# Two heads per value product, part of an output product in split precision, and two copies moved from ScalarE to VectorE

## The chip, the cores and the metric

The kernel runs on one core of a Trainium2 chip. The metric is the device time of one execution in microseconds; the time before is 1042.04 us, the median of three runs (1040.24 to 1042.3).

## The reference

Three stages follow one another. Attention: 4 batches, 8 heads, 576 positions, head dimension 64, with a mask by blocks of 64 (a query sees its own block and those before it).

```python
scores = scale * q @ k.T                      # masked where block_i < block_j
attn = softmax(scores)
x = (attn @ v) -> (2304 tokens, 512)
h = x @ w_in                                  # 512 -> 2048
x2 = (h - tanh(h)) @ w_out                    # 2048 -> 512
xn = x2 / rms(x2) * rms_g
out = (silu(xn @ w_gate) * (xn @ w_val)) @ w_out2     # 512 -> 1536 -> 512
```

## The kernel before, in words

The 2304 tokens are six groups of 384. Most products are made in *split parts*: each operand is the sum of a high and a low part of type fp32r, and three products (high by high, high by low, low by high) take the place of one product of float32 operands (`gemm_out`, L704 to L707). The weights arrive as 64-bit numbers and are turned into float32 words on ScalarE and VectorE (`convert`, L129 to L151): for split parts it also makes the high part (ScalarE, `rnd`, L102) and the low part (VectorE, `lo`, L107).

Attention comes in units: one batch and its first six or last three query blocks, times four pairs of heads. The units of groups 0 and 1 are *light*: they use plain float32 operands. A pair of heads passes through score steps ("s", `scores`: product L481, maximum L494 on VectorE, exponential L496 on ScalarE), transposes of the probabilities ("t", `transp`: L525 on TensorE, then a copy into `pp`, which is on VectorE for every third tile of unit 0 and on ScalarE for the others), and value products ("a", `av_light`, L570 to L584): for each head three products of 64 columns of weights with 384, 256 and 128 columns of probabilities (L578). Head 0 writes partitions 0 to 63 of a bank `t`, head 1 partitions 64 to 127. After the second head ScalarE copies the bank to `xh` and VectorE makes `xl`. A float32 product shows as two records in the trace.

Unit 0, the first batch, runs alone in the first 50 us, since the first hidden product needs its result; a few conversions of weights (EARLY, L650 on) are mixed in. From then on the steps of the next unit are put between the matrix products of the current group (`aslot`, L908 on, by a table of costs in `plan`, L366 to L391), so that unit 1 runs beside group 0, unit 2 and others beside group 1.

Each group walks 16 chunks of 128 hidden columns: hidden product L929 to L931 (12 products), tanh on ScalarE (L937), `gh`, and the output product `out1` (L710 to L724) into three accumulators one chunk later in group 0 and LAG = 2 chunks later in the other groups. Group 0's output product uses float32 operands (L715), one product per tile of 128 tokens instead of three. Its output weights are converted to float32, two chunks in one ring tile, and stored (w1f, L648); group 1 loads them again, splits them (`w1get`, L664 to L674, ScalarE `w<-st` and VectorE) and stores the split parts (w1d), which groups 2 to 5 load. TensorE's order is that of the code; on the other engines a scheduler orders the instructions.

## Time and profile before

| | before |
|---|---|
| median of three runs | 1042.04 us |
| the profiled execution's own time | 1042.98 us |
| its span, first to last instruction | 1041.1 us |
| mean granted TensorE clock | 0.996 |
| TensorE busy | 98% |
| VectorE, ScalarE, GpSimd busy | 71%, 64%, 33% |

Busy times of matmuls are sums of intervals whose ends are modelled and overlap; the distance between two starts tells how long TensorE was held. Idle time of an engine costs something only where another engine waits for it.

### The profile page before, as it was taken

Reading aid. Unit: us, or ns where it says so; the run is one execution under the profiler, and the core shown is the slowest. Engines: PE = TensorE matmul, PEld = TensorE weight load, DVE = VectorE, ACT = ScalarE, POOL = GpSimd, SP = SyncE. Lnnn points to the kernel's source line nnn. Section 1 sums busy time; section 2 is a strip of 40 time slices with the busy share of each in tenths; the row PEclk is TensorE's granted clock in tenths of the full one; section 3 lists DMA queues with packets and bytes.
Section 4 is the critical chain, followed back from the end, with each engine's and each line's share of the span. In section 5 each row is a group of like instructions: output and inputs, shape, how many; then the busy total and the mean of one; then the engine's idle time right before and its main releaser. Section 6 shows DMA issues by size and latency. Waiting matters only on the chain.

```text
span 1041.1 us, 17914 instructions
## 1 busy us (share of the span) xinstructions
PE 1023.0 (98%) x6014; PEld 934.2 (90%) x6014; DVE 736.3 (71%) x1489; ACT 666.3 (64%) x1533; POOL 342.9 (33%) x467
## 2 busy tenths in 40 slices
PE   8899999999999999999999999999999999999998
PEld 5676668999899989999999989999999999999998
DVE  5776558676777786668666988837866678666775
ACT  6877768787898887788868776624732247412253
POOL 5522111122343233324332624645211370111710
PEclk9999999999999999999999999999999999999999
DMA  9998799979787699857859989986697667876664
GB/s 224 269 340 267 252 280 274 287 219 265 222 234 199 152 267 292 229 188 256 294 161 365 383 321 355 347 324 248 225 331 295 247 217 260 287 297 236 250 231 134
DMA packets 190957, 274.03 MB, mean 263 GB/s; under 512 B 109456, under 2 KB 151184, under 8 KB 184464
## 3 DMA queue, kind: packets, MB, share of 16 engines
q1 hardware_dynamic: 190864, 272.87, 80.1%
q8 instruction: 48, 0.79, 0.3%
q14 instruction: 45, 0.37, 0.1%
HBM read 209.39 MB, written 63.44 MB: 262 GB/s over the span
## 4 chain that ended last, share of the span: by engine, by line
PE 86%; DVE 5%; ACT 4%; DMA 2%; issue 1%; POOL 1%; SPq 1%; DVEq 0%; ACTq 0%; POOLq 0%
PE t L929 6%; PE t L931 6%; PE t L930 5%; PE t L481 5%; PE gv L1026 5%; PE gv L1027 5%; PE gv L1025 5%; PE acc L705 4%; PE acc L707 4%; PE acc L706 4%; PE acc L715 4%; PE t L525 4%; PE ga L1025 3%; PE ga L1027 3%; PE ga L1026 3%; PE ga L707 2%
## 5 line engine op out<-in xcount | busy, mean ns | idle before, releaser
L929 PE MATMUL t<-xh,w 128*128 128x384 f32 x384 | 137.1, 357 | 0.1
L931 PE MATMUL t<-xh,w 128*128 128x384 f32 x384 | 129.6, 338 | 0.0
L930 PE MATMUL t<-xl,w 128*128 128x384 f32 x384 | 129.3, 337 | 0.0
L1027 PE MATMUL gv<-xh,ws 128*128 128x384 f32 x308 | 103.4, 336 | 0.0
L1026 PE MATMUL gv<-xl,ws 128*128 128x384 f32 x308 | 103.4, 336 | 0.0
L1025 PE MATMUL gv<-xh,ws 128*128 128x384 f32 x308 | 103.3, 336 | 0.0
L705 PE MATMUL acc<-w,gh 128*128 128x512 f32 x240 | 98.5, 410 | 0.4 <-DVE x2s L723 0.2
L496 ACT ACTIVATE pt<-pt,stat 128x64 f32<-128x64 f32 (+2 forms) x144 | 80.5, 560 | 26.8 <-DVE pt L494 26.3
L707 PE MATMUL acc<-w,gl 128*128 128x512 f32 x240 | 94.8, 395 | 0.3 <-DVE gl L107 0.3
L706 PE MATMUL acc<-w,gh 128*128 128x512 f32 x240 | 94.4, 393 | 0.0
L1079 ACT ACTIVATE gt<-c 128x384 f32<-128x384 f32 x29 | 15.3, 527 | 119.6 <-DVE c L1078 119.6
L494 DVE TENSOR_SCALAR_CACHE_REDUCE pt<-t 128x64 f32<-128x64 f32 (+2 forms) x144 | 64.2, 451 | 28.2 <-PE t L481 26.8
L1082 POOL TENSOR_TENSOR g<-va,vb 128x384 f32<-128x384 f32 x29 | 31.1, 1073 | 154.3 <-ACT va L1081 137.7
L929 PEld LDWEIGHTS t<-xh,w 128*128 128x128 f32 x384 | 72.3, 188 | 4.1 <-issue 0.7
L930 PEld LDWEIGHTS t<-xl,w 128*128 128x128 f32 x384 | 72.4, 189 | 2.3
L931 PEld LDWEIGHTS t<-xh,w 128*128 128x128 f32 x384 | 72.0, 188 | 0.0
L102 ACT ACTIVATE pp<-t 128x512 fp32r<-128x512 f32 (+6 forms) x152 | 63.4, 436 | 11.5 <-PE t L525 10.8
L525 PE MATMUL t<-ident,pt 128*128 128x128 f32 x400 | 65.6, 273 | 1.8 <-DVE xl L107 1.3
L107 DVE TENSOR_TENSOR pp<-t,pp 128x512 fp32r<-128x512 f32 (+3 forms) x112 | 55.2, 509 | 16.3 <-ACT pp L102 15.7
L107 DVE TENSOR_TENSOR gl<-gt,gh 128x384 fp32r<-128x384 f32 x80 | 53.9, 673 | 18.0 <-ACT gh L102 17.7
L525 PEld LDWEIGHTS t<-ident,pt 128*128 128x128 f32 x400 | 50.5, 140 | 16.0 <-issue 5.2
L107 POOL TENSOR_TENSOR vp<-vr,vp 128x640 fp32r<-128x640 f32 (+1 forms) x24 | 33.2, 1383 | 86.0 <-ACT vp L102 86.0
(209 smaller groups left out, 3123.0 us busy)
## 6 DMA issues: line engine op xcount, KB each, us to landing
ws<-w2d SPq DMA_DIRECT2D x26, 1792.0 KB, 7.3
w<-w1d_i SPq DMA_DIRECT2D x68, 512.0 KB, 5.1
ws<-wod SPq DMA_DIRECT2D x21, 1536.0 KB, 6.0
w<-w1d_o SPq DMA_DIRECT2D x52, 512.0 KB, 5.3
st<-in_moe_w_out SPq DMA_DIRECT2D x28, 512.0 KB, 5.0
w2d<-wc SPq DMA_DIRECT2D x9, 1024.0 KB, 7.5
st<-in_moe_w_in SPq DMA_DIRECT2D x16, 512.0 KB, 5.3
w1d_i<-w SPq DMA_DIRECT2D x16, 512.0 KB, 4.3
```

The costliest lines, as they stand in the source:

```text
L107: eng.tensor_tensor(out=o, in0=full, in1=hi.bitcast(F32), op=ALU.subtract)
L496: ACT.activation(out=pt[:, 0:keys], in_=pt[:, 0:keys], func=AF.Exp, scale=-1.0, bias=least, accum_out=st[:, 8 + ti:9 + ti])
L525: PE.transpose(t[:, (j - a) * 128:(j - a + 1) * 128], pt[:, j * 128:(j + 1) * 128], ident)
L705: PE.matmul(acc, lhsT=gh[:, c], rhs=wh, start=first, stop=False, skip_group_check=more)
L706: PE.matmul(acc, lhsT=gh[:, c], rhs=wl, start=False, stop=False, skip_group_check=more)
L707: PE.matmul(acc, lhsT=gl[:, c], rhs=wh, start=False, stop=last, skip_group_check=more)
L929: PE.matmul(h, lhsT=wh[:, c], rhs=xh[:, kk], start=(kk == 0), stop=False)
L930: PE.matmul(h, lhsT=wh[:, c], rhs=xl[:, kk], start=False, stop=False)
L931: PE.matmul(h, lhsT=wl[:, c], rhs=xh[:, kk], start=False, stop=(kk == KD - 1))
L1025: PE.matmul(ps, lhsT=wh[:, c], rhs=xh[:, kk], start=(first and kk == 0), stop=False)
L1026: PE.matmul(ps, lhsT=wh[:, c], rhs=xl[:, kk], start=False, stop=False)
L1027: PE.matmul(ps, lhsT=wl[:, c], rhs=xh[:, kk], start=False, stop=(last and kk == nk - 1))
```

## The change

Three edits. (1) A light value step is one step for both heads: the products of the two heads alternate, head 0 and head 1 for each block of 128 keys, into one bank. (2) With SPLIT = 12, chunks 12 to 15 of group 0 use split parts in the output product: their output weights are converted with high and low part, one chunk per ring tile, and stored as split parts at once; the activation is split as well, and the lag is 2 chunks there. Group 1 loads these four chunks' weights instead of splitting them. (3) In unit 0 the copies of tiles 2 and 5 of each pair go from ScalarE to VectorE.

```diff
--- before.py
+++ after.py
@@ -51,6 +51,7 @@
 JH = J2 // 2
 MIXED = range(3, 10)
 LAG = 2
+SPLIT = 12
 AVLEAD = 3
 
 
@@ -377,7 +378,7 @@
                     period.setdefault(m, ([], [], []))[0].extend(("s", i, t) for t in half)
                     period.setdefault(m + 2, ([], [], []))[1].extend(("t", i, t) for t in half)
                     m += 1
-                period.setdefault(m + 2, ([], [], []))[2].extend(("a", i, hh) for hh in range(2))
+                period.setdefault(m + 2, ([], [], []))[2].extend(("a", i, hh) for hh in range(1 if u.light else 2))
             for n in sorted(period):
                 sc, tr, av = period[n]
                 self.seq += sc[0:2] + av + tr[0:1] + sc[2:3] + tr[1:]
@@ -386,7 +387,7 @@
                 u = self.pairs[n][0]
                 if kind == "a":
                     self.end[u.group] = m + 1
-                self.cost.append(self.cost[-1] + (u.tiles[t][0] + 150 if kind in "st" else 400))
+                self.cost.append(self.cost[-1] + (u.tiles[t][0] + 150 if kind in "st" else 800 if u.light else 400))
             self.pos = 0
 
         def goal(self, g):
@@ -525,7 +526,7 @@
                     PE.transpose(t[:, (j - a) * 128:(j - a + 1) * 128], pt[:, j * 128:(j + 1) * 128], ident)
                 tv = t[:, 0:(z - a) * 128].rearrange("p (j h c) -> p j h c", h=2, c=64)
                 if u.light:
-                    rnd(ACT if u.group or ti % 3 else DVE, hv[:, a:z].bitcast(F32), tv)
+                    rnd(ACT if u.group or ti % 3 == 1 else DVE, hv[:, a:z].bitcast(F32), tv)
                 else:
                     rnd(ACT, hv[:, a:z], tv)
                     lo(DVE, lv[:, a:z], tv, hv[:, a:z])
@@ -536,7 +537,8 @@
             vp = d.get("vp")
             self.events.add(("a", i, hh))
             if u.light:
-                return self.av_light(u, p, hh, d)
+                self.events.add(("a", i, 1))
+                return self.av_light(u, p, d)
             o = env["t"].tile([128, 512], F32, name="t", tag="t")
             if hh == 0:
                 d["xs"] = at.tile([128, TG], F32, name="xs", tag="xs", bufs=1)
@@ -567,21 +569,18 @@
                 rnd(ACT, hv, xs[:, 0:nq])
                 lo(POOL, xl[:, p, u.off:u.off + nq], xs[:, 0:nq], hv)
 
-        def av_light(self, u, p, hh, d):
+        def av_light(self, u, p, d):
             nq = u.nq
-            if hh == 0:
-                d["o"] = env["t"].tile([128, 512], F32, name="t", tag="t")
-            o = d["o"]
-            xa = slice(64 * hh, 64 * hh + 64)
+            o = env["t"].tile([128, 512], F32, name="t", tag="t")
             for j in range(u.nb):
-                src, s = u.cols(d["pp"], hh, 0, j)
-                PE.matmul(o[xa, s:nq], lhsT=d["v"](j, hh), rhs=src.bitcast(F32),
-                          start=(j == 0), stop=(j == u.nb - 1))
-            if hh:
-                xh, xl = xt("A", u.group)
-                hv = xh[:, p, u.off:u.off + nq]
-                rnd(ACT, hv, o[:, 0:nq])
-                lo(DVE, xl[:, p, u.off:u.off + nq], o[:, 0:nq], hv)
+                for hh in range(2):
+                    src, s = u.cols(d["pp"], hh, 0, j)
+                    PE.matmul(o[64 * hh:64 * hh + 64, s:nq], lhsT=d["v"](j, hh), rhs=src.bitcast(F32),
+                              start=(j == 0), stop=(j == u.nb - 1), skip_group_check=True)
+            xh, xl = xt("A", u.group)
+            hv = xh[:, p, u.off:u.off + nq]
+            rnd(ACT, hv, o[:, 0:nq])
+            lo(DVE, xl[:, p, u.off:u.off + nq], o[:, 0:nq], hv)
 
     att = Attn()
     staged = {}
@@ -637,6 +636,11 @@
                 convert(staged.pop(n), t[:, 0:512], t[:, 512:1024])
                 SP.dma_start(out=w1d[0][j], in_=t.bitcast(F32))
                 wi[j] = t
+                return
+            if j >= SPLIT:
+                t = wo[j] = w1tile(1, j)
+                convert(staged.pop(n), t[:, 0:512], t[:, 512:1024])
+                SP.dma_start(out=w1d[1][j], in_=t.bitcast(F32))
                 return
             if j % 2 == 0:
                 wo["new"] = w1tile(1, j + 1, F32)
@@ -650,7 +654,7 @@
         fstaged = {}
 
         def stagef(m):
-            if m < J1 // 2:
+            if m < SPLIT // 2:
                 fstaged[m] = env["stg"].tile([128, 1024], F32, name="st", tag="st")
                 SP.dma_start(out=fstaged[m], in_=w1f[m])
 
@@ -663,7 +667,7 @@
             t = wi[s] = w1tile(0, until(s))
             SP.dma_start(out=t.bitcast(F32), in_=w1d[0][j])
             t = wo[s] = w1tile(1, until(s))
-            if g == 1:
+            if g == 1 and j < SPLIT:
                 f = fstaged[j // 2][:, 512 * (j % 2):512 * (j % 2) + 512]
                 rnd(ACT, t[:, 0:512], f)
                 lo(DVE, t[:, 512:1024], f, t[:, 0:512])
@@ -711,7 +715,7 @@
             if j == 0:
                 accs[t] = accp.tile([128, DM], F32, name=f"acc{t}", tag=f"acc{t}")
             gh, gl = gts[s]
-            if g == 0:
+            if s < SPLIT:
                 PE.matmul(accs[t], lhsT=gh[:, t * 128:t * 128 + 128], rhs=wo[s], start=(j == 0), stop=(j == J1 - 1))
             else:
                 gemm_out(accs[t], gh, gl, wo[s][:, 0:512], wo[s][:, 512:1024], t, j == 0, j == J1 - 1)
@@ -936,7 +940,7 @@
             gt = wk.tile([128, TG], F32, name="gt", tag="gt")
             ACT.activation(out=gt, in_=h, func=AF.Tanh)
             gl = None
-            if g == 0:
+            if s < SPLIT:
                 gh = wk.tile([128, TG], F32, name="gh", tag="gh", bufs=3)
                 DVE.tensor_tensor(gh, h, gt, ALU.subtract)
             else:
@@ -948,7 +952,7 @@
             aslot()
             gts[s] = (gh, gl)
             pend.append(s)
-            if len(pend) > (LAG if g else 1):
+            if len(pend) > (LAG if s >= SPLIT else 1):
                 n = pend.pop(0)
                 out1(n, 0)
                 aslot()
```

Lines of the changed kernel are 1 to 4 higher than those of the same code before. The order of instructions moves at three places.

TensorE, second batch (unit 1), first pair of heads, between a transpose of queries (qt) and the first output products (L715, acc). In the kernel before:

```order
L578 MATMUL t<-pp,vp 64x384
L578 MATMUL t<-pp,vp 64x256
L578 MATMUL t<-pp,vp 64x128
L929 MATMUL t<-xh,w_745 128x384
L930 MATMUL t<-xl,w_745 128x384
L931 MATMUL t<-xh,w_745 128x384
L929 MATMUL t<-xh,w_745 128x384
L930 MATMUL t<-xl,w_745 128x384
L931 MATMUL t<-xh,w_745 128x384
L715 MATMUL acc_864<-w_668,gh 128x512
L578 MATMUL t<-pp,vp 64x384
L578 MATMUL t<-pp,vp 64x256
```

In the changed kernel:

```order
L578 MATMUL t<-pp,vp 64x384 x2
L578 MATMUL t<-pp,vp 64x256 x2
L578 MATMUL t<-pp,vp 64x128 x2
L933 MATMUL t<-xh,w_745 128x384
L934 MATMUL t<-xl,w_745 128x384
L935 MATMUL t<-xh,w_745 128x384
L933 MATMUL t<-xh,w_745 128x384
L934 MATMUL t<-xl,w_745 128x384
L935 MATMUL t<-xh,w_745 128x384
L719 MATMUL acc_864<-w_663,gh 128x512
L719 MATMUL acc_866<-w_663,gh 128x512
L719 MATMUL acc_868<-w_663,gh 128x512
```

The six value products of both heads stand together and alternate (x2 is one product of each head); before, a half hidden product and an output product stood between the heads.

VectorE, first batch, first pair: maxima of scores (L494, before; L495, changed), copies of probabilities (pp) and a conversion of weights (cv, w). Before:

```order
L494 TENSOR_SCALAR pt,stat<-t 128x192
L494 TENSOR_SCALAR pt,stat<-t 128x256
L505 RECIPROCAL stat<-stat 128x3
L143 TENSOR_SCALAR cv<-cv 128x512
L494 TENSOR_SCALAR pt,stat<-t 128x320
L144 SCALAR_TENSOR_TENSOR cv<-cv,cu 128x512
L104 COPY pp<-t 128x2x2x64
L494 TENSOR_SCALAR pt,stat<-t 128x384
L494 TENSOR_SCALAR pt,stat<-t 128x64
```

In the changed kernel:

```order
L495 TENSOR_SCALAR pt,stat<-t 128x192
L105 COPY pp<-t 128x2x2x64
L495 TENSOR_SCALAR pt,stat<-t 128x256
L506 RECIPROCAL stat<-stat 128x3
L144 TENSOR_SCALAR cv<-cv 128x512
L495 TENSOR_SCALAR pt,stat<-t 128x320
L145 SCALAR_TENSOR_TENSOR cv<-cv,cu 128x512
L105 COPY pp<-t 128x2x2x64
L495 TENSOR_SCALAR pt,stat<-t 128x384
L105 COPY pp<-t 128x3x2x64
L108 TENSOR_TENSOR w_310<-cv,w_310 128x512
```

Two copies to pp are new on VectorE: one of 2x2x64 ahead of the 256-wide maximum, and one of 3x2x64 behind the 384-wide maximum, the copy of the last tile of the pair.

ScalarE, end of group 0: w<-st is the split of output weights for group 1, gt the tanh, gh the high part of the activation, xh the copy of the value products' bank. Before:

```order
L102 ACTIVATE w_1617<-cv 128x512
L496 ACTIVATE pt,stat<-pt,stat 128x384
L102 ACTIVATE w_1680<-st 128x512
L102 ACTIVATE w_1759<-st 128x512
L937 ACTIVATE gt<-t 128x384
L504 ACTIVATE stat<-stat 128x3
L102 ACTIVATE pp<-t 128x3x2x64 x2
L512 ACTIVATE pt<-pt,stat 128x256
L512 ACTIVATE pt<-pt,stat 128x320
L512 ACTIVATE pt<-pt,stat 128x384
```

In the changed kernel:

```order
L103 ACTIVATE w_1645<-cv 128x512
L941 ACTIVATE gt<-t 128x384
L497 ACTIVATE pt,stat<-pt,stat 128x64
L103 ACTIVATE kh<-t 128x384
L103 ACTIVATE qh_131<-t 64x6x64
L497 ACTIVATE pt,stat<-pt,stat 128x128
L103 ACTIVATE qh_131<-t 64x6x64
L103 ACTIVATE gh<-gt 128x384
L103 ACTIVATE w_1690<-st 128x512
L103 ACTIVATE xh<-t 128x384
L103 ACTIVATE vp<-vr 128x6x64
L941 ACTIVATE gt<-t 128x384
```

The split for chunk 16 (w_1690) stands behind the tanh of chunk 14 and its gh, and ahead of xh of the last light pair and of the tanh of chunk 15. Before, the first two splits stood ahead of a tanh.

## Rows read from the trace of the kernel before

**Rows 1.** Stretches: us, PE, PEld, DVE, ACT, POOL busy (x), PEclk, DMA share, GB/s.

```profile
20.00:50.00 30.00, 25.77 (x146) 17.75 (x145) 21.99 (x77) 25.30 (x83) 17.20 (x38) 0.89 1.01 281
50.00:165.00 115.00, 115.00 (x534) 81.84 (x534) 72.99 (x178) 85.61 (x217) 20.01 (x43) 1.00 0.88 284
165.00:325.00 160.00, 158.21 (x923) 144.80 (x922) 118.51 (x305) 133.96 (x356) 46.10 (x72) 1.00 0.87 246
```

**Rows 2.** Longest wait of TensorE, 0 to 330 us: total us, times, longest.

```profile
PE t L578 <- ACT pp L102: 4.1, 4, 1.7
```

**Rows 3.** Chain of waits up to 52 us: start us, us, what.

```profile
29.33 0.39 ACT pp L102
29.75 3.87 PE t L578 x11
...
38.57 0.59 ACT pt L496 x2
...
45.55 0.75 ACT pp L102 x2
...
46.35 2.23 PE t L578 x11
```

**Rows 4.** TensorE in order of time, one head of the second batch (start us, us).

```profile
66.83 1.51 PE L578 MATMUL t<-pp,vp 128*64 128x384 f32 x6
68.27 0.44 PE L929 MATMUL t<-xh,w 128*128 128x384 f32 x1
```

**Rows 5.** TensorE in order of time, first and third block of the first batch.

```profile
19.72 3.88 PE L578 MATMUL t<-pp,vn 128*64 128x384 f32 x12 [1.47 <-ACT pp L102]
23.52 0.33 PE L525 MATMUL t<-ident,pt 128*128 128x128 f32 x1
...
38.63 2.21 PE L578 MATMUL t<-pp,vn 128*64 128x384 f32 x12 [0.50 <-ACT pp L102]
40.77 0.33 PE L525 MATMUL t<-ident,pt 128*128 128x128 f32 x1
```

**Rows 6.** TensorE's records in flight at 39.50 us.

```profile
L578 PE MATMUL t<-pp,vn 128*64 128x384 f32 x1 | 0.5, 537 | 0.0
L578 PE MATMUL t<-pp,vn 128*64 128x256 f32 x1 | 0.4, 379 | 0.0
```

**Rows 7.** TensorE in order of time, output product of one chunk, group 0.

```profile
103.29 2.74 PE L715 MATMUL acc<-w,gh 128*128 128x512 f32 x6
105.87 0.70 PE L481 MATMUL t<-kh,qf 128*128 128x320 f32 x2
```

**Rows 8.** The same in group 1, in split parts: first products of two tiles, next work.

```profile
183.86 0.48 PE L705 MATMUL acc<-w,gh 128*128 128x512 f32 x1
...
184.64 0.39 PE L705 MATMUL acc<-w,gh 128*128 128x512 f32 x1
...
185.33 0.19 PE L481 MATMUL t<-kh,qh 128*128 128x64 f32 x1
```

**Rows 9.** Groups of ScalarE and VectorE, 50 to 165 us: busy us, mean ns, idle before.

```profile
L102 ACT ACTIVATE w<-cv 128x512 fp32r<-128x512 f32 x13 | 8.2, 631 | 2.6 <-DVE cv L144 2.4
...
L102 ACT ACTIVATE w<-st 128x512 fp32r<-128x512 f32 x4 | 2.4, 624 | 3.0 <-PE acc L715 2.7 <-DMA st<-w1f 0.3
...
L102 ACT ACTIVATE gh<-gt 128x384 fp32r<-128x384 f32 x2 | 1.0, 511 | 0.0
...
L107 DVE TENSOR_TENSOR w<-cv,w 128x512 fp32r<-128x512 f32 x13 | 9.3, 715 | 5.9 <-ACT w L102 5.7
```

**Rows 10.** The stretch of the second block, columns as in rows 1.

```profile
29.99:33.40 3.41, 3.41 (x12) 1.83 (x10) 1.25 (x3) 1.42 (x6) 2.27 (x4) 0.50 1.12 278
```

**Rows 11.** Copies of probabilities by width, 10 to 50 us: busy us, mean ns.

```profile
L102 ACT ACTIVATE pp<-t 128x384 f32<-128x384 f32 x8 | 3.6, 475 | 0.0
...
L102 ACT ACTIVATE pp<-t 128x256 f32<-128x256 f32 x4 | 1.5, 373 | 0.0
...
L104 DVE COPY pp<-t 128x256 f32<-128x256 f32 x4 | 1.7, 417 | 0.0
```

## The prediction

> **What bounds the kernel now.** TensorE is busy 98% of the span, but an average hides stages, so I read the table by stretch first. From 50 us on TensorE has next to no idle time (115.00 busy of 115, 158.21 of 160), while from 20 to 50 us it is idle for 4.2 of 30 [rows 1]. The list of waits says what stands in front of it there: its longest wait, 4.1 us in 4 pieces, is that of the light value products (L578) for ScalarE's copies of probabilities [rows 2]. So two rules of sum hold. After 50 us each TensorE microsecond removed shortens the kernel, as long as the other engines keep up. Before 50 us only what lies on the chain of waits counts: that chain passes through the second and the fourth block of value products, but at the time of the third (38.6 to 40.8) through ScalarE's exponentials [rows 3]; the first block waits for its copy like the second [rows 5].
>
> A busy row for matmuls counts durations that overlap, so I price TensorE's work by the distance between starts.
>
> **Value products of the second batch (after 50 us).** There are 8 blocks, one per head, of 6 records (each float32 product is two). One block takes from 66.83 to the next instruction at 68.27: 1.44 us [rows 4]. A pair of heads costs 2.88. What does one block cost in which both heads alternate, each filling half of the array's columns? The trace of before answers at the seam between the two heads of the first batch, where twelve records stand together: 38.63 to 40.77 is 2.14 us, not 2.88 [rows 5]. So 0.74 us of the two went on at once. At 39.50 a product over 384 columns and one over 256 are in flight and none over 128 [rows 6]: head 0, in the middle of its 1.44, is at its 256, so the 384 is head 1's, in the other half of the columns. Neither head seems slowed: counted back from 40.77, head 1's 1.44 begin at 39.33, when half of head 0's (to 40.07) are over. In the new order (first place shown with the change: 384 x2, 256 x2, 128 x2) the halves alternate from the first record, so I take 1.44 for both heads. Saved: 4 x (2.88 - 1.44) = **5.8 us**. Bounds: 0 if alternating halves undo the overlap, and 5.8, since one head alone takes 1.44.
>
> **Output products of chunks 12 to 15.** A chunk's three float32 products (six records) take 103.29 to 105.87, 2.58 us [rows 7]. In split parts the three products of one tile take 0.78 after a transpose (183.86 to 184.64) and 0.69 otherwise (to 185.33) [rows 8]. A chunk is then 2.07 to 2.34; I take one such switch per chunk, 2.16. Saved 4 x 0.42 = **1.7 us**, bounds 1.0 and 2.0. Beside it each of these chunks gives ScalarE the high part of weights and activation (0.63 + 0.51) and VectorE the low parts (0.72, and by width an estimated 0.54) [rows 9]. I cost that at nothing: from 50 to 165 us ScalarE is busy 85.6 and VectorE 73.0 of 115 [rows 1]; four chunks of 7.2 us (115 / 16) leave ScalarE 7 idle us for 4.6, VectorE 10 for 5.0. With that cover gone it would cost up to 4 x 2.4 = 9.6. Group 1 is rid of four of its splits, which hide behind TensorE. The longer lag removes nothing: chunk 12's output moves behind chunk 14's hidden product, and the next group starts with two chunks pending instead of one.
>
> One wait is added. The ring's output tiles are now taken singly, so chunk 16's weights go into chunk 12's tile, and ScalarE's w<-st stands there until TensorE is through with chunk 12 (third place shown with the change). The nearest row is the same instruction before, which waited 2.7 us once [rows 9]. Queued behind it on ScalarE are the copy of the last light pair (xh), which chunk 16's hidden product needs, and chunk 15's tanh. TensorE has by then the hidden product of chunk 15 and the output of chunk 13 ahead of it: three products over 384 columns by the 512 of [rows 8] are 0.69 x 384 / 512 = 0.52, four times that 2.1, and 2.1 + 2.16 = 4.2 us, more than the 2.7. So 0, with 2.7 as the bound. On SyncE four stores of split weights take the place of two float32 ones in group 0, and in group 1 four loads that of four stores and two loads; the bytes balance, at DMA shares of 0.88 and 0.87 [rows 1]. POOL gets nothing new.
>
> **The first 50 us.** The same interleaving shortens four blocks. The first takes 3.81 us (19.72 to 23.52) [rows 5], the second as long on the chain [rows 3], at half clock: granted 0.50, that is 1.2 GHz, from 29.99 to 33.40 [rows 10], after TensorE had stood waiting (1.47 us ahead of the first block [rows 5]). Scaled from the warm seam, 1.44 x 3.81 / 2.14 = 2.56, so 1.25 each, 2.5 together. The fourth saves 2.14 - 1.44 = 0.7. The third does too, but the chain there runs on ScalarE [rows 3], so 0. The copies: two per pair go from ScalarE to VectorE, 256 wide (0.373) and 384 wide (0.475), 3.4 us in four pairs; VectorE pays 0.417 and, by ScalarE's ratio of the two, an estimated 0.53 [rows 11]. On the chain they are the last piece ahead of a block: 0.39 at 29.33, half of the 0.75 for two at 45.55 [rows 3], at most 1.5 for four. The last two copies now run side by side, but VectorE's is longer and stands behind a 384-wide maximum (second place); and VectorE, 22.0 us busy of 30, gains 2.8 in the three pairs from 20 to 50 us, while ScalarE falls from 25.3 to 22.8 [rows 1]. With the DMA engines at a share of 1.01 in that stretch, weights can hardly land earlier for the conversions that ScalarE does in between. So of the 1.5 I keep 0.4. Sum 2.5 + 0.7 + 0.4 = **3.6 us**; bounds 1.2 (one block, the rest taken up by conversions that wait for weights) and 5.4 (all four blocks and all of the 1.5).
>
> **Sum.** 5.8 + 1.7 + 3.6 = 11.1 us from the profiled execution's 1042.98 (its span 1041.1 plus 1.9 around it): 1031.9. The median of the three runs lies 0.94 lower, so **1030.9**. All terms at their good ends, 13.2, give 1028.8.
>
> **Rivals.** (a) *Starts in program order.* If no product may start before all ahead of it have, the halves run in lockstep. In parts of 128 columns a head's records are 3, 3, 2, 2, 1, 1; if each starts after the one ahead of it has started and its own half is free, both heads end after 15 parts instead of 12: 1.44 x 15 / 12 = 1.80 us. Then 4 x 1.08 = 4.3 in the second batch, and 0.61 + 0.61 + 0.34 plus the copies' 0.4 = 2.0 in the first: with the 1.7, 8.0 saved, 1034.0. Against it: head 1's 384 was in flight at 39.50 before head 0's 128s had started, which stand ahead of it in the program [rows 6]. The Trainium skill (TensorE: Matmul & The Clock Gate, Part 3: Packing small matmuls — row/col tiling) states this order as a rule: matmuls start and end in program order, and only weight loads are pulled ahead. By that rule the time would be 1034.0; the trace does not agree with it at this seam.
>
> (b) *The first stretch is bound elsewhere.* Conversions and full DMA engines [rows 1] take up what the blocks free, 1.2 instead of 3.6: 1033.3. For it: the DMA share of 1.01. Against: the last pieces on the chain ahead of the blocks are copies, not transfers [rows 3].
>
> (c) *No overlap when halves alternate.* The blocks cost what they did; 1.7 and the copies' 0.4 remain: 1039.9. Against it: the seam [rows 5, 6].
>
> (d) *Slower.* ScalarE and VectorE become the bound in chunks 12 to 15. Price: the splits of these chunks, 9.6 if nothing covers them, and the wait for a ring tile, 2.7 at each of chunks 16 to 19, 10.8. All of it on TensorE's path is 20.4, against 11.1 gained: 9.3 more than before, 1051.3. It turns the sign once over 55% of it (11.1 / 20.4) reaches TensorE. Against it: in group 1 ScalarE is busy 134 of 160 with such splits in each chunk, and TensorE idles 1.8 [rows 1].
>
> **How the numbers follow.** Forecast 0.66, (a) 0.10, (b) 0.13, (c) 0.05, (d) 0.04, and 0.02 for a change in the scheduler's later order that cancels it all. The range reaches from the best ends, 1028.8 less 1.0 for the spread of the runs shown, to 1035.5, where (a) and (b) meet with the 1.0 of the split products (4.3 + 1.2 + 1.0 = 6.5 saved); (c) and (d) lie outside. A difference of 0.2%, 2.1 us, is about what a measurement of this kernel can tell from none. Rival (c), 2.1 below the median, sits on that line: of its 0.05 I count 0.02 as the same, and half of the unexplained 0.02. So same 0.03; slower is (d), 0.04; faster is the rest, 0.93.
>
> **What would show it.** Blocks of L578 with 12 records that take some 1.44 us to the next start in the second batch (1.80 for (a), 2.9 for (c)); the first hidden product about 3.6 us earlier; nine records in about 2.2 us for each output of chunks 12 to 15; TensorE as full as before from there on, and no new wait of TensorE for ScalarE's w or gh. The prediction is wrong if a block of both heads takes over 2 us, or if TensorE shows idle microseconds between 130 and 190.

## The result, and the profile after

The changed kernel takes **1031.15 us** (median of 4 runs, 1029.03 to 1032.66) against 1042.12 of the kernel before on the same chip (4 runs, 1040.24 to 1042.3): ratio 0.9897, 95% interval 0.9875 to 0.992, faster by 11.0 us. The forecast was 1030.9, in the range 1027.8 to 1035.5. The profiled execution took 1029.03 us, with a span of 1027.2 and a mean granted clock of 0.999; TensorE is busy 98% of it, VectorE 72%, ScalarE 65%.

The sum came out within 0.3 us, but not each of its terms: that is what most of the experiments are about. The stretches of the changed kernel, columns as in [rows 1]:

```profile
20.00:50.00 30.00, 25.20 (x174) 19.69 (x171) 28.18 (x94) 27.14 (x87) 19.45 (x42) 1.00 1.09 300
50.00:165.00 115.00, 114.39 (x597) 88.38 (x596) 83.85 (x205) 95.39 (x246) 21.51 (x43) 1.00 0.95 312
130.00:190.00 60.00, 59.39 (x346) 53.24 (x346) 43.29 (x114) 48.37 (x137) 10.63 (x18) 1.00 0.95 296
150.00:160.00 10.00, 9.39 (x61) 8.43 (x60) 8.47 (x22) 8.74 (x24) 2.17 (x3) 1.00 1.08 364
```

Three things differ from [rows 1]. From 20 to 50 us the granted clock is 1.00 instead of 0.89. VectorE rose from 22.0 to 28.2 there; ScalarE rose from 25.3 to 27.1, since more of the work that follows now lies inside the same 30 us: counted up to the first hidden product, ScalarE fell from 37.5 us (of 50.16) to 34.8 (of 44.45), and VectorE rose from 32.2 to 34.6. And TensorE, which had no idle time from 50 to 165, now has 0.6 us, all of it between 150 and 160. The waits of TensorE from 52 to 330 us (total, times, longest) name it:

```profile
PE t L482 <- DVE pp L108: 1.4, 1, 1.4
PE acc L709 <- DVE x2s L727: 0.8, 2, 0.6
```

The first row belongs to a later unit and both kernels have it. The second is new: the first output product of group 1 waits until VectorE has read group 0's accumulators (`x2s`). The chain of waits from 140 to 160 us shows why:

```profile
147.91 0.70 DVE x2s L727
148.63 5.55 DMA x2d<-x2s
154.21 0.70 DVE x2s L727
154.95 0.50 PE acc L709
```

Group 0 ends with three reads of accumulators, one per tile of 128 tokens, into a ring of two `x2s` buffers (which `cu`, a step of the weight conversions, shares), and each is then stored. The third read stands until the first store has landed, 5.55 us, and TensorE behind it.

TensorE in order of time, the blocks of value products (first, second and last block of the first batch; first of the second batch) and the first hidden product (start, us, line, shapes; x12 is six products of two records each; in brackets the wait ahead):

```profile
19.11 1.52 PE L578 MATMUL t<-pp,vn 128*64 128x384 f32 x12 [1.49 <-ACT pp L103]
20.55 0.33 PE L526 MATMUL t<-ident,pt 128*128 128x128 f32 x1
...
26.50 1.52 PE L578 MATMUL t<-pp,vn 128*64 128x384 f32 x12
27.94 0.33 PE L526 MATMUL t<-ident,pt 128*128 128x128 f32 x1
...
41.15 1.51 PE L578 MATMUL t<-pp,vn 128*64 128x384 f32 x12 [1.07 <-ACT pt L497]
...
44.45 0.47 PE L933 MATMUL t<-xh,w 128*128 128x384 f32 x1
...
61.13 1.51 PE L578 MATMUL t<-pp,vp 128*64 128x384 f32 x12
62.58 0.44 PE L933 MATMUL t<-xh,w 128*128 128x384 f32 x1
62.86 0.34 PE L934 MATMUL t<-xl,w 128*128 128x384 f32 x1
```

A block of both heads takes 1.44 to 1.45 us from its start to the next (19.11 to 20.55, 26.50 to 27.94, 61.13 to 62.58), as long as one head did before [rows 4]. The last block of the first batch has a wait behind it, so its length does not show.

Output product of one chunk, in split parts, with a score product between the first two tiles:

```profile
139.97 0.48 PE L709 MATMUL acc<-w,gh 128*128 128x512 f32 x1
...
140.75 0.28 PE L482 MATMUL t<-kh,qh 128*128 128x256 f32 x1
...
141.10 0.40 PE L709 MATMUL acc<-w,gh 128*128 128x512 f32 x1
...
142.48 0.31 PE L482 MATMUL t<-kh,qh 128*128 128x320 f32 x1
```

Nine records take 0.78 + 1.38 = 2.16 us (140.75 - 139.97 and 142.48 - 141.10), against 2.58 in [rows 7]: the value taken in the prediction.

**Where the time came from.** The start of the same hidden product in both traces, chunk by chunk (before minus after):

| hidden product (from 0) | before | after | difference |
|---|---|---|---|
| 0 | 50.16 | 44.45 | 5.7 |
| 4 | 73.93 | 66.60 | 7.3 |
| 8 | 100.29 | 91.34 | 8.95 |
| 12 | 127.08 | 116.47 | 10.6 |
| 31, the last of group 1 | 238.27 | 225.08 | 13.2 |
| end of the span | 1041.11 | 1027.21 | 13.9 |

The first stretch gives 5.7. Each pair of heads gives 1.63 (three pairs between chunks 0 and 12, 4.9; with the fourth 6.5). What is left up to 13.2 is the split output products less the wait for `x2s`: 13.2 - 5.7 - 6.5 = 1.0. The last 0.7 lies behind the last hidden product, which the change does not touch; the experiments' profiles have 0.2 to 1.2 of it against this profile of before too, so the change is not needed for it. This pair of executions is 13.95 us apart, while the medians are 11.0 apart; the experiments say why.

### The profile page after: what moved, and what is told of

Read it like the earlier page. It is cut to its first block, busy times and chain, and to the rows that moved or that the text cites. A ratio compares the mean times of both kernels' runs of the same rounds, so it can differ in the third digit from the quotient of the medians.

```text
span 1027.2 us, 17940 instructions
## 1 busy us (share of the span) xinstructions
PE 1008.6 (98%) x6026; PEld 930.4 (91%) x6026; DVE 739.5 (72%) x1501; ACT 663.9 (65%) x1529; POOL 343.8 (33%) x467
## 4 chain that ended last, share of the span: by engine, by line
PE 89%; DVE 4%; DMA 3%; ACT 2%; issue 1%; SPq 1%; POOL 0%; DVEq 0%; POOLq 0%
PE t L933 6%; PE t L935 6%; PE t L934 6%; PE t L482 6%; PE gv L1031 5%; PE gv L1029 5%; PE gv L1030 5%; PE acc L709 5%; PE acc L711 5%; PE acc L710 5%; PE t L526 3%; PE ga L1031 3%; PE ga L1029 3%; PE ga L1030 3%; PE acc L719 3%; PE ga L711 2%
## 5 line engine op out<-in xcount | busy, mean ns | idle before, releaser
L709 PE MATMUL acc<-w,gh 128*128 128x512 f32 x252 | 103.3, 410 | 1.0 <-DVE x2s L727 0.8
L711 PE MATMUL acc<-w,gl 128*128 128x512 f32 x252 | 99.6, 395 | 0.3 <-DVE gl L108 0.3
L710 PE MATMUL acc<-w,gh 128*128 128x512 f32 x252 | 99.2, 393 | 0.0
L495 DVE TENSOR_SCALAR_CACHE_REDUCE pt<-t 128x64 f32<-128x64 f32 (+2 forms) x144 | 63.8, 449 | 23.1 <-PE t L482 21.8
L947 DVE TENSOR_TENSOR gt<-t,gt 128x384 f32<-128x384 f32 x84 | 46.2, 550 | 27.6 <-ACT gt L941 27.3
L103 ACT ACTIVATE pp<-t 128x512 fp32r<-128x512 f32 (+5 forms) x144 | 60.7, 436 | 7.7 <-PE t L526 6.9
```

The lines of the kernel that those rows point to most:

```text
L709: PE.matmul(acc, lhsT=gh[:, c], rhs=wh, start=first, stop=False, skip_group_check=more)
L710: PE.matmul(acc, lhsT=gh[:, c], rhs=wl, start=False, stop=False, skip_group_check=more)
L711: PE.matmul(acc, lhsT=gl[:, c], rhs=wh, start=False, stop=last, skip_group_check=more)
```

## Experiments

### One edit at a time (e1 to e3)

e1 has only the common step of both heads, e2 only the split parts, e3 only the copies. Against the changed kernel:

```diff
 e1
-SPLIT = 12
+SPLIT = 16
-                    rnd(ACT if u.group or ti % 3 == 1 else DVE, hv[:, a:z].bitcast(F32), tv)
+                    rnd(ACT if u.group or ti % 3 else DVE, hv[:, a:z].bitcast(F32), tv)
 e2
-                period.setdefault(m + 2, ([], [], []))[2].extend(("a", i, hh) for hh in range(1 if u.light else 2))
+                period.setdefault(m + 2, ([], [], []))[2].extend(("a", i, hh) for hh in range(2))
...
-                return self.av_light(u, p, d)
+                return self.av_light(u, p, hh, d)
...
 e3
-            if j >= SPLIT:
...
+                return self.av_light(u, p, hh, d)
```

(e2 keeps the value steps and the copies of the kernel before, e3 its value steps and output products.)

> Only the value products of both heads in one alternating step; output products and copies as before. My theory: each of the four blocks of the second batch takes 1.45 us with 12 records, and each pair of heads gives 1.6 us of distance between the same hidden products (6.5 in all); the first stretch gives another 2.5 to 4.5, since the blocks there stand on the chain with or without the copies. So 9 to 11 us below the kernel before: 1031 to 1033. Rival 1, the first stretch's gain came from the copies: 5.8 to 6.5 below, 1035.5 to 1036.5. Rival 2, the split output products carried a good part: the second batch then gives under 5.

> Only the split output products of chunks 12 to 15 of group 0. My theory: TensorE saves 4 x 0.25 to 0.5 us at these chunks and loses next to nothing to waits, so 1.0 to 1.7 us below the kernel before: 1040.4 to 1041.1, inside what can be told from no change. Rival, the splits on ScalarE and VectorE and the wait for the ring tile reach TensorE: up to 9.6 us more than before, seen as idle time of TensorE between 130 and 175 us.

> Only the two more copies of probabilities per pair on VectorE in the first batch. My theory: the first hidden product starts 0.4 to 1.5 us earlier than at 50.16 us and nothing changes behind it: 1040.5 to 1041.7. Rival 1, the copies carry the first stretch's gain of 5.7 us: 1036 to 1038. Rival 2, VectorE becomes the bound of the first stretch: first hidden product at or behind 50.2, 1042 to 1043.

| | us, median (runs) | ratio to before (95%) | first hidden product |
|---|---|---|---|
| before, beside them | 1041.1 (23) | | 50.16 |
| e1, heads | 1033.01 (6) | 0.9923 (0.9906 to 0.9941) | 45.15 |
| e2, split parts | 1038.70 (12) | 0.9978 (0.9967 to 0.9989) | 46.97 |
| e3, copies | 1038.72 (12) | 0.9983 (0.9971 to 0.9994) | 45.87 |

The three gains, 8.0, 2.3 and 1.8 us by the ratios, add up to 12.1; the whole change gave 10.7 with an interval of 8.3 to 13.0. So the times show no large interaction between the edits; a small one would lie inside these intervals, and the profiles below show two (the wait for `x2s`, and copies that are worth less on top of the blocks than alone). Against the expectations, e1 gained less than its 9 to 11, and e2 and e3 somewhat more than theirs (1.0 to 1.7; 0.4 to 1.5), though their intervals reach into them.

e2 holds the surprise: it changes nothing ahead of the first hidden product, where its instructions stand in the order of before, and yet it reaches that product 3.2 us earlier. Its first stretch (columns as in [rows 1]):

```profile
20.00:50.00 30.00, 25.89 (x165) 19.38 (x164) 24.49 (x83) 27.55 (x91) 18.02 (x40) 1.00 1.07 299
```

and TensorE in order of time up to its first hidden product:

```profile
46.64 0.30 PE L526 MATMUL t<-ident,pt 128*128 128x128 f32 x1 [1.26 <-DVE xl L108]
46.78 0.49 PE L482 MATMUL t<-kh,qf 128*128 128x192 f32 x2
46.97 0.48 PE L935 MATMUL t<-xh,w 128*128 128x384 f32 x1
```

The clock is 1.00 throughout. In the profile of before two stretches were granted 0.50: that of the second block [rows 10], and, by the same view, that of the first:

```profile
19.70:23.20 3.50, 3.48 (x10) 1.88 (x11) 1.72 (x6) 2.98 (x10) 1.69 (x4) 0.51 1.20 246
```

Two blocks of 3.81 instead of 2.14 are 3.3 us, the 3.2 that e2 is ahead. The waits ahead of the blocks are much the same (ahead of the first 1.47 in before [rows 5] and in e2; ahead of the second 1.67 and 1.51), so whether the clock falls there differs from execution to execution, with the same order of instructions. (Variants of the changed kernel met such a stretch in their first 50 us as well: e4, e7 and e12.) At like clock the reference for the first hidden product is 46.97, and the edits give there: heads 1.8 (45.15), copies 1.1 (45.87), both 2.5 (44.45).

From there on e1 gains 1.63 per pair as the whole change does, up to hidden product 18. Then it loses 0.6 (11.5 ahead of before at 18, 10.9 at 20), about half of it a wait of 0.32 for VectorE's `pp` at 155.05: the earlier end of group 0 meets a wait in e1 too, without any split product. e3 gains nothing (4.3 us ahead of before at chunk 0 and 4.3 at chunk 40). e2 is 3.2 ahead at chunk 12 and 4.8 at the end of group 1: the split parts alone are worth 1.6, not the 1.0 that they bring within the change. e4, below, has the same left: of the 9.15 that it is ahead at hidden product 31, 3.78 are there at 0 and 3.74 are the pairs', so 1.63 remain. In e2 and e4 TensorE's waits from 150 to 170 us have none for `x2s`. In e1 a half-clock stretch at 254 us took back 1.3 (10.7 ahead of before at chunk 35, 9.4 at chunk 40, the chunks counted on through the groups).

### One step, but head after head (e4)

The same six products in one step, in the order of before.

```diff
-            for j in range(u.nb):
-                for hh in range(2):
+            for hh in range(2):
+                for j in range(u.nb):
```

> The changed kernel with one step for both heads, but head 0's three products ahead of head 1's three instead of alternating. My theory: the overlap depends on how early head 1's first product is reached, so a block takes 2.14 us as at the seam of the first batch before, against 1.45: 4 x 0.7 = 2.8 us in the second batch and 0 to 2 in the first more than the changed kernel, 1034 to 1036. Rival, it is enough that both heads stand together: blocks of 1.45 and the time of the changed kernel, 1031.

1034.26 us (6 runs), ratio 0.9937 (0.9921 to 0.9952). TensorE in order of time:

```profile
63.05 2.21 PE L578 MATMUL t<-pp,vp 128*64 128x384 f32 x12
65.19 0.44 PE L933 MATMUL t<-xh,w 128*128 128x384 f32 x1
```

The block takes 2.14 us, as at the seam of [rows 5]. Its records in flight from 63.92 to 63.95 us have the shapes of [rows 6]:

```profile
L578 PE MATMUL t<-pp,vp 128*64 128x384 f32 x1 | 0.5, 537 | 0.0
L578 PE MATMUL t<-pp,vp 128*64 128x256 f32 x1 | 0.4, 379 | 0.0
```

Head 0's products over 384 are over by then (half of its 1.44 us), so the 384 is head 1's, and it runs before head 0's products over 128 have started. A pair gains 0.93 instead of 1.63: 2.88 - 2.14 = 0.74, and the same 0.19 on top that e1 and the whole change have over 2.88 - 1.44. So the order alone is worth 0.70 per pair, and putting the heads into one step 0.93. The 0.19 is the cost of a second entry to and exit from such a block: 0.11 is seen at the exit, where the first hidden product holds TensorE for 0.28 (62.58 to 62.86 above) and later ones for 0.17, and 0.09 at the entry, where before's output product ahead of head 1 holds it for 0.95 (69.42 to 70.37) and others for 0.86 (2.58 / 3 [rows 7]). e4's time is in its expected range, 1034 to 1036.

### Extra matmuls ahead of the blocks (e5, e6)

To separate the clock from the work: four products of zeros ahead of each block of the first batch, in the kernel before (e5, ahead of head 0) and in the changed one (e6), so that TensorE does not stand idle there.

```diff
+            if u.group == 0:
+                for n in range(4):
+                    PE.matmul(o, lhsT=zero[:, 0:128], rhs=zero[:, 0:512], start=True, stop=True)
             for j in range(u.nb):
```

> The kernel before with four extra matmuls of zeros (bf16, 128x512, into the bank of the block) ahead of each value block of the first batch, so that TensorE does not stand idle there. My theory: the scatter of the kernel before comes from stretches of half clock (granted 0.50) after TensorE waits ahead of these blocks; with the extra matmuls they stay away, the mean clock of the runs is 0.999 or 1.0, blocks take 2.14 us instead of 3.81, and the median is that of the kernel before's own runs at 0.999, 1039.3, some 1.8 below its median. Rival 1, the clock has no part in it: nothing moves or the extra work costs up to 4 x 0.9 us: 1041 to 1044.5. Rival 2, the clock stays up but the first stretch is held by ScalarE, so the first hidden product stays near 50 us.

> The changed kernel with the same extra matmuls. My theory: no stretch of half clock in the first 50 us, blocks of 1.45 us in every run, median that of the changed kernel's runs at 0.999 and above, 1029.0 to 1030.4, against 1031.15. If the predicted 3.6 us of the first stretch rested on blocks at half clock, the difference between this and the kernel before with the same matmuls is smaller in the first stretch, 1 to 3 us, and about 8 to 9.5 in all. Rival: the matmuls delay the blocks, 1032 to 1034.

e5: 1041.1 (12 runs), before beside it 1040.53 (17), ratio 1.0003 (0.9993 to 1.0013). e6: 1031.8 (4), ratio 0.9912 (0.9898 to 0.9926). In both profiles the first stretch has full clock, and e6's four runs have a mean clock of 0.999 or 1.000. But the extra matmuls hold up the blocks. e6's first one:

```profile
18.59 1.02 PE L577 MATMUL t<-zero 128*128 128x512 bf16 x3 [0.50 <-DVE pp L105]
19.58 1.51 PE L581 MATMUL t<-pp,vn 128*64 128x384 f32 x12
```

(Three of the four have a record.) The block starts at 19.58 instead of 19.11, and after four blocks the first hidden product is at 46.43 instead of 44.45. e5 has it at 48.56, 1.6 later than e2 at the same clock. My expectation that e5 would gain fell: what the clock gives back, the fill takes (e5's profile also met a half-clock stretch later, at 262.7 us, which took 1.4). e6 missed its 1029.0 to 1030.4 too. In its profile the fill is not all of that: it is 2.0 behind the changed kernel at the first hidden product, and loses another 1.8 at the end of group 1, where TensorE waits for `x2s` (1.55 us at 360.94). What e6's expectation said of the difference between the two filled kernels held: 2.1 us in the first stretch (1 to 3 expected), 9.3 by the medians (8 to 9.5).

### Fewer conversions in the first stretch (e7)

The chain of the changed kernel passes there through a load of weights and the conversions behind it, "27.29 6.07 DMA st<-in_moe_w_in", then ScalarE's `cv` at 33.38. With EARLY 4 instead of 7 fewer of them stand there.

```diff
-EARLY = 7
+EARLY = 4
```

> The changed kernel with 4 instead of 7 weight conversions (EARLY) mixed into the first batch. My theory: in the first stretch ScalarE's conversions and the transfers they wait for are what is left on the chain, so the first hidden product comes 1.5 to 3 us earlier than at 44.45; group 0 has three more conversions, which fit beside TensorE, so 1028.5 to 1030. Rival: the conversions are missing at the start of group 0 and TensorE waits for weights there, as much or more than was won: 1031 to 1035.

1029.5 us (4 runs), ratio 0.9891 (0.9876 to 0.9906). The first hidden product comes 0.9 earlier (43.52). At chunk 20 the lead is gone:

```profile
154.97 0.50 PE L709 MATMUL acc<-w,gh 128*128 128x512 f32 x1 [1.58 <-DVE x2s L727]
```

Its first store of `x2s` takes 6.52 us on the chain (5.55 in the changed kernel), and TensorE starts the same product at 154.97, where the changed kernel has it at 154.95. So the wait for the store hides what is gained ahead of it. The median is in the expected range, but not by the mechanism expected: 0.9 us came instead of 1.5 to 3, the profiled executions of e7 and of the changed kernel are only 0.1 us apart, and what the 1.65 between the medians rests on cannot be told from four runs each.

### Split parts in twice as many chunks (e8)

Rival (d) in small: four more chunks gain 0.42 each, or ScalarE and VectorE become the bound.

```diff
-SPLIT = 12
+SPLIT = 8
```

> The changed kernel with SPLIT = 8: chunks 8 to 15 of group 0 in split parts. My theory: each further chunk saves TensorE 0.4 us as chunks 12 to 15 do, 1.6 in all, if ScalarE can carry 1.1 us more in chunks 8 to 11, where it still does two conversions per chunk of 6 us: 1029.5. Rival, ScalarE and VectorE become the bound: TensorE idles between 90 and 125 us, and the kernel is up to 4 x 2.4 = 9.6 us slower than without cover, 1031 to 1039.

1036.37 us (5 runs), ratio 0.9953 (0.994 to 0.9966): 5.2 us **slower** than the changed kernel. Two stretches:

```profile
100.00:120.00 20.00, 20.00 (x113) 16.31 (x112) 17.22 (x39) 19.55 (x49) 5.46 (x9) 1.00 0.93 271
130.00:140.00 10.00, 7.69 (x38) 5.71 (x39) 7.12 (x16) 8.34 (x23) 1.99 (x3) 0.83 1.03 418
```

and TensorE's waits from 52 to 330 us:

```profile
PE acc L709 <- DVE x2s L727: 2.4, 2, 2.2
PE t L482 <- ACT pp L103: 1.7, 1, 1.7
```

ScalarE is full from 100 to 120 us (19.55 of 20). The chain of waits runs there from 99.9 to 122.3 through ScalarE and VectorE by turns, then through a load of output weights for 6.24 us at 122.27. TensorE is idle for 2.3 us between 130 and 140 and runs at half clock for a stretch there, and the end of the group waits 2.2 us for `x2s`, this time behind ScalarE's work and not behind a store. At hidden product 8, the first that the edit touches, e8 is 2.3 us behind the changed kernel (its first products ran slowly: three transposes at 10.27 took 0.85 us, in the changed kernel at 8.28 0.49; the granted clock shown for both is 1.00, and the reason stays open), at the end of group 1 6.4 behind: 4.1 lost where 1.6 should have been won. From 50 to 165 us its TensorE is idle for 4.2 us more than the changed kernel's. (In between, at 12, it is 1.3 ahead, but one output product is still to come there because of the longer lag.) That ScalarE is the cause is read from its busy time and the chain; no run separates it from VectorE or from the load. The time lies in the rival's range.

### A third buffer for x2s (e9 to e12)

The third `x2s` takes a buffer of the ring of conversions (`cv`) instead of waiting for the first store. e10 adds EARLY 4, e12 EARLY 2, e11 EARLY 4 and SPLIT 10.

```diff
-    env["x2s"] = lambda g, t: wk.tile([128, DM], F32, name="x2s", tag="x2s")
+    env["x2s"] = lambda g, t: wk.tile([128, DM], F32, name="x2s", tag="cv" if t == 2 else "x2s")
 e10, e11
-EARLY = 7
+EARLY = 4
 e11
-SPLIT = 12
+SPLIT = 10
 e12
-EARLY = 7
+EARLY = 2
```

> The changed kernel, with the third result tile of a group (x2s, third tile of tokens, groups 0 and 1) in another pair of buffers, so that VectorE does not wait at the end of group 0 for the store of the first tile to land. My theory: this wait (VectorE 0.5 us for the DMA, TensorE 0.6 behind it at 154.95 us) is what keeps the split output products at 1.0 instead of 1.6 us; without it TensorE does not idle between 150 and 160 us, and the second chunk of group 1 onward comes 0.6 to 0.8 us earlier: 1030.4 against 1031.15. Rival: VectorE itself is late there (its splits), TensorE's wait stays at 0.5 or more and the time is the same.

> The same with 4 conversions in the first batch instead of 7. My theory: the 0.9 us that EARLY = 4 won ahead of group 0 was lost again at the same wait (1.6 us there); with both the gain is kept, so 1.5 to 2.5 us below the changed kernel: 1028.7 to 1029.7, and below the run with EARLY = 4 alone. Rival: the loss moves on to the next wait, 1029.5 as with EARLY = 4 alone.

> The same as the run before with SPLIT = 10, two more chunks in split parts. My theory from SPLIT = 8: where chunks still convert weights, ScalarE has no room left; two more chunks of splits win 0.8 on TensorE and lose more to waits for weights, so 0 to 3 us slower than the run with SPLIT = 12: 1029 to 1032.5. Rival: chunks 10 and 11 still fit and it is 0.8 us faster.

> Third result tile in its own buffers, and 2 conversions in the first batch. My theory: the first stretch shortens by another 1 to 2 us against EARLY = 4, but group 0 now has 30 conversions to do in 14 chunks and its first chunks wait for weights; as much is lost: 1028.5 to 1031. Rival: conversions fit beside group 0 and it is the fastest, 1027 to 1028.5.

| | us, median (runs), lowest to highest | ratio to before (95%) |
|---|---|---|
| before, beside them | 1041.81 (9) | |
| e9, third buffer | 1029.86 (5), 1028.71 to 1031.51 | 0.9889 (0.9872 to 0.9907) |
| e10, and EARLY 4 | 1028.68 (4), 1028.12 to 1029.29 | 0.9876 (0.986 to 0.9892) |
| e11, and SPLIT 10 | 1028.39 (5), 1028.02 to 1031.29 | 0.9881 (0.9864 to 0.9898) |
| e12, EARLY 2 | 1029.58 (4), 1027.79 to 1030.08 | 0.9882 (0.9864 to 0.9899) |

The wait is gone in e9. The three tiles of group 1's first output product follow each other, where the third of the changed kernel stood 0.61 us:

```profile
153.53 0.45 PE L709 MATMUL acc<-w,gh 128*128 128x512 f32 x1
...
154.27 0.39 PE L709 MATMUL acc<-w,gh 128*128 128x512 f32 x1
...
154.96 0.93 PE L560 MATMUL t<-pp,vp 128*128 128x384 f32 x6
```

Up to chunk 18 e9 is 0.1 behind the changed kernel, from chunk 19 on 0.8 ahead: 0.9 for the buffer, by which the split parts come to 1.0 + 0.9 = 1.9, against 1.6 in e2 and in e4 and 1.7 in the prediction. In e2 and e4 hidden product 19 follows 18 by 7.46 us, in e9 by 7.17, so up to 0.3 of what the end of the group loses is still in theirs. At 251 us this execution met a half-clock stretch that took 1.5 back, so the time shows no difference that the runs can tell.

e10 keeps 0.6 of EARLY 4's gain at the first hidden product (43.82), loses 0.9 at chunk 15, and gains 0.9 from the buffer. What is late next is a copy of probabilities on ScalarE, around 130 us (TensorE's waits from 52 to 330 us):

```profile
PE t L246 <- ACT pp L103: 0.7, 1, 0.7
```

All four runs of e10 lie below three of the four of the changed kernel, and it is the best version here by its ratio; but its interval overlaps that of the change. e11 and e12 show no further gain in time. In e11 TensorE is idle for 1.0 us between 100 and 110 us; even so it is 1.1 us ahead of e10 at the end of group 1 (0.6 of it from the first stretch), and loses 1.5 right behind that, at the same kind of wait, one group later:

```profile
357.24 0.50 PE L709 MATMUL acc<-w,gh 128*128 128x512 f32 x1 [1.20 <-DVE x2s L727]
```

There the third read of `x2s` stands 2.08 us for the first store, although the third buffer is in. e10 has no such wait there. e12 is 0.8 us ahead of e10 at the first hidden product and 1.0 behind at the third: its first chunks wait for weights, as expected (0.71 us for ScalarE's `w` at 46.92, 0.54 for VectorE's at 48.07). So the cover for split parts is worn thin at SPLIT 10 and gone at SPLIT 8. e12 is in its expected range; e9, e10 and e11 came out a little below theirs.

## Why the prediction was right, point by point

- **"From 50 us on each TensorE microsecond removed shortens the kernel"**: right. Blocks and split products arrive at the end of group 1 in full, save for the wait there (0.9, e9).
- **Second batch, 5.8**: 6.5. The block of both heads takes 1.45 as read off the seam. The 0.7 too little is the entry and exit of a block, four fewer of them, which the distance within one block doesn't hold (e4 has the same 0.19 per pair). The term was right in its mechanism and too small in size.
- **Rival (a), starts in program order**: fell; the block took 1.45, not 1.80. The 1.80 takes the order record by record. Taken product by product (a float32 product is two records), the order holds nothing up where the halves alternate, and 1.45 would fit; so that block alone does not refute it. Head after head does (e4): in program order head 1 could not start before head 0's products over 128, 10 of head 0's 12 parts on, so the block would take an estimated 1.44 x 10 / 12 + 1.44 = 2.64 us, and it took 2.14, with head 1's 384 in flight ahead of head 0's 128s. The Trainium skill (TensorE: Matmul & The Clock Gate, Part 3: Packing small matmuls — row/col tiling) states that matmuls start and end in program order; e4's block, and the seam of [rows 5, 6], do not agree with it for the two halves of the columns.
- **Split output products, 1.7**: 1.0 in the change, 1.6 alone (e2, e4), 1.9 with the wait taken away (e9). The price per chunk was right, 2.16. The term was too large by the new wait for `x2s`, which the prediction did not look for: it asked what each chunk gives ScalarE and VectorE, and not whether the end of the group, now 12 us earlier, still meets a store of `x2s` (a median of 2.1 to 7.9 us to land in four profiles). Its own sign of being wrong, idle microseconds between 130 and 190, did appear, with 0.6 us.
- **"One wait is added ... so 0"** (ring of output tiles): right. The group of ScalarE's w<-st from 50 to 165 us (busy, mean ns, idle before):

```profile
L103 ACT ACTIVATE w<-st 128x512 fp32r<-128x512 f32 x6 | 3.8, 630 | 1.2 <-PE acc L711 1.1
```

  It stood 1.1 us for the output product, less than the 2.7 of [rows 9], and no wait of TensorE for `w` or `gh` appeared.
- **First 50 us, 3.6**: 5.7 in this pair of profiles, 2.5 at like clock. The term was built on two blocks at half clock, as the profile of before showed them; the changed kernel's profile had none. So 3.2 of the 5.7 are the clock, and the changed kernel cannot count on them. The mechanism held at like clock: the chain of e2, at full clock, passes through the first, second and fourth block and not through the third (start us, us, what), and these three at 0.7 each with the 0.4 of the copies would have given 2.5.

```profile
19.75 2.21 PE t L579 x11
...
28.19 2.21 PE t L579 x11
...
43.16 2.23 PE t L579 x11
```

  Taken alone they divide otherwise: of the blocks 1.8 arrive (e1 against e2: 0.14 ahead of them, 0.34 of the first, 0.68 of the second, 0.02 of the third, 0.64 of the fourth), and the copies are worth 1.1 alone (e3), 0.7 on top of the blocks. Rival (b) shows in part: in the changed kernel the chain passes through a load of weights at 27.29, for which ScalarE stands 0.82 us; what that takes is not shown.
- **Rival (c)**: fell with the blocks. **Rival (d)**: fell for SPLIT 12. For SPLIT 8 (e8) the cover is gone, with ScalarE full as it said; e8 is slower than the changed kernel, but still faster than before.
- **The sum.** At like clock the parts are 6.5 + 1.0 + 2.5 = 10.0. The runs are consistent with that: three runs of before beside e1 to e4 had a mean clock of 0.999, median 1039.3; the two of the changed kernel at 0.999 and 1.000 took 1029.03 and 1030.37, on the mean 9.6 less, and the two kernels with extra matmuls differ by 9.3 (e5, e6). The mean clock is a rough guide only: e7's run at 1.000 was the slowest of its four. Eleven runs of before at 0.997 had a median of 1042.5. That the forecast of 11.1 met the 11.0 of the medians is in part luck: it counted from a profile with two half-clock stretches (1042.98), and three of the four runs of before beside the changed kernel lie near it, at 1042.0 to 1042.3. The terms missed by +0.7, -0.7 and, at like clock, -1.1. How the rest of the medians' difference divides into clock and chance cannot be told from four runs.

## What to carry to other kernels

Two matmuls that each fill half of the array's columns went on side by side in full where the program alternates between the halves, and for a third of the block (0.74 of 2.14 us) where one half follows the other; a seam between two such blocks in an old trace showed the overlap before it was built. Before a block at half clock is counted as gained or lost, look at a second execution with the same order of instructions: here the clock of a stretch differed from run to run, and 3 us of difference between two profiles were the clock alone. When everything ahead of a group's end gets earlier, look at the ring buffers behind its stores: what was just in time becomes the next wait.

## What the runs showed of the hardware that was not expected

- Twelve records of two heads in alternation take 1.45 us, one head alone 1.44 [rows 4]: no slowing of one half by the other shows, although both write the same bank `t`.
- Between the first products and the last three microseconds, the granted clock fell to 0.50 (1.2 of 2.4 GHz) in one or two stretches of some profiled executions (before, e1, e4, e5, e7, e8, e9, e12) and in none of others (the changed kernel, e2, e3, e6, e10, e11); before and e2 have the same instructions and much the same waits ahead of the place. Two in the first 50 us cost 3.2 us, one at 254 us (e1) 1.3. TensorE had stood waiting a little earlier: 1.47 us ahead of the first block, 1.39 for VectorE's `pp` at 250.6 in e1; the changed kernel has the same waits (1.49 at 19.11, 1.4 for `pp`) and kept the full clock.
- Four products of zeros ahead of each block were followed by full clock in the first 50 us of both profiles (before's own profile had 0.89 from 20 to 50 us, e2's 1.00 without them), and e5's median is no lower than before's beside it (1041.1, 1040.53).
- The same three stores of `x2s`, 256 KB each, took a median of 2.1 us to land in before and in e2, but 4.6 in the changed kernel and 7.9 in e9, where the DMA engines' share is 1.08 and 1.03 from 150 to 160 us. Which transfers they met there stays open.
